# Layer A's query softmax sums and denominators from one pass of products, and whole-array transposes for the last block's output

## The chip, the cores and the metric

The kernel runs on one NeuronCore of a Trainium2 chip. Its five engines have queues of their own and meet only through semaphores: PE (TensorE, matrix products into eight PSUM banks), DVE (VectorE), ACT (ScalarE), POOL (GpSimd) and SP (SyncE, which issues nearly all DMAs). An instruction at the head of a queue that waits holds up everything behind it on that engine. The metric is the device time of one execution in microseconds (us); lower is better.

## The reference

The input x has 2048 rows of 512 values. Four residual layers follow one another, A, B, A, B, each x = x + layer(layernorm(x)), with 32 heads of 16 values.

Layer A is linear attention with softmax features:

```python
pq = einsum(q, w_phi); pk = einsum(k, w_phi)
phi_q = concat([softmax(pq), softmax(-pq)]); phi_k = concat([softmax(pk), softmax(-pk)])
kv = einsum("bhsf,bhsd->bhfd", phi_k, v);  z = einsum("bhsf->bhf", phi_k)
den = einsum("bhqf,bhf->bhq", phi_q, z) + 1e-6
o = einsum("bhqf,bhfd->bhqd", phi_q, kv) / den;   out = o @ wo
```

Layer B is local attention: each position looks at 8 positions behind it, two apart, and its output goes through a second matrix `wo`.

Write E0 = exp(pq) and E1 = exp(-pq), S0 and S1 for their sums over a head's 16 features, and D0 and D1 for their sums weighted by z. The denominator is D0/S0 + D1/S1, and what multiplies E0 is rho0 = 1 / (S0 (D0/S0 + D1/S1)). The same number is S1 / (D0 S1 + D1 S0).

## The kernel before

The rows are cut into four blocks of 512 (b = 0 to 3), each of four tiles of 128 (t = 0 to 3); L is 0 or 1 for the first or second pair of layers. The work is written as stages, named for layer, L and b, and each stage is a list of small steps, one list per engine:

- `fold1`, `fold0`: w_phi is folded into the key and query weights at the start (wT holds transposed weights).
- `lnA0..`: first layer norm. `stat` is statistics on VectorE (line 514), `ap` the normalisation, `pt` and `pe` transposes on PE and their copies.
- `a1_Lb` (lines 615 to 690): key products `mk`, exponentials `ek` on ScalarE, value products `mv`, sums over features, normalisation, and `kv`, which adds into one PSUM bank over all four blocks.
- `a2_Lb` (lines 720 to 743): query products `mq`, the exponentials `eq` (E0 and E1 in tiles Eq), then `ms` (32 small products with the 0/1 matrix indS give S0 and S1) and `rs` (their reciprocals by Ln and Exp into rS).
- `akvL` (lines 760 to 779): the copy of kv, four transposes `tr`, and from them ZM (z, spread over 32-column regions) and R. This is the point at which layer A has seen all keys; no denominator can start before it.
- `a3_Lb` (lines 800 to 860): `md`, 32 small products of Eq and ZM, give D0 and D1; `dr` on VectorE multiplies them with rS and adds; `ln` on ScalarE takes the reciprocal (Ln, Exp); `rho` multiplies it with rS. Then rho is spread over the features, for four blocks by small products `bc` with indB and multiplied into Eq (`mulp`, line 838), for the other four through DRAM (`wr`, `rdb`, `muld`).
- `a4_Lb`: numerators (line 923), output product with WoA (line 542), residual sum and norm. A residual sum is done either on VectorE (line 555) or by a fifth product with the identity on PE (545) and a copy on ScalarE (552).
- `b1`, `b2`, `b3`: layer B, with products on VectorE over shifted windows (`prod`, line 1042, and `pav`, line 1104, four of each for a block), sums on PE, and Vg, copies of V that SP's DMAs spread over the partitions.
- The last block of the last layer (L = 1, b = 3) does layer B another way, on PE: `sc`, `mo`, `nrm`, then `b4_13.pt`, which transposes its output with 64 products onto 32-column strips (line 1365), and the output product with WoB, whose rows were loaded in a matching permuted order.

Which step is issued when is not computed in the kernel. A string, `_ORDER`, lists step after step as base-36 numbers of the lists; each number issues the next step of that list. A second string, `_CHOICE`, says for each flexible step (a PSUM eviction, a normalisation, a residual sum) which engine does it, and `_SLOTS` which buffer each tile takes. What made them is not in the file. The constants that GpSimd makes (line 210 on: masks, cleared ZM tiles, ones) are issued ahead of the string and are not in it. Each engine then executes its own instructions strictly in the order of the string.

Of the kernel before, what the change touches and what calls it, by code (L numbers as in the profile page):

```python
# [8 lines left out]
BF16 = mybir.dt.bfloat16  # L9
# [7 lines left out]
P = 128  # L17
NJ = 16
D = 512
# [31 lines left out]
    "rho_pad": 0,  # L51
# [9 lines left out]
8 2 i 2e 3s e3 ce 2p 23 i a 5l i i 9 i i i 5o i i i i 4e e7 1m i 0 3u 3r 0 f i e c j b 2 k 3 4 j o 5q 1m l 3 m  # L61
p 1n 0 i 1 n 1t e4 o 1o q 1m 1p r 0 1m 1u s 1m z 5k z z 5 1m 1r 7 6 z 20 20 7 1q 1s 1t 21 21 t 20 20 1v 22 10
z 22 1t 7 1t 20 1w 22 t 11 24 24 13 u 12 16 12 1t t 15 1t v 12 12 22 x 18 14 1x d w w 1y 2c y 18 18 26 18 2d
1f 2d 2c 1z 2d 24 2d 27 17 19 18 1a 1b 21 1c 1d 22 21 22 39 1e 20 20 22 39 25 2c 3b 3a 3a 1f 3a 2d 3a 2f 2c 1f
1f 39 ch 22 2f 2d 2g 1g 29 1f 2d 1j 2f 2d 7 1h 29 1i 1k 3a 29 2n 29 2i 2n 3c 2o 2o 2o 2k 2o 2k 2q 1l cd 2h 2n
2a 2k 2f 2n 2k 3a 2o 2j 24 2q 2r 2q 2o 2o 2o 29 2y 28 2y 2y 3c 2l 2z 2v 2z 2s 2z 2z 2k 2y 2z 39 36 31 2z 36 2z
3a 3b 36 36 2v 31 2v 37 2v 31 2t 36 2z 36 2b 2b 2b 2b 2m 2m ci 36 36 2m 3a 2w 2m 2v 33 34 32 31 3c 35 2q 3c 36
3b 2x g 2x 2u 2x 30 37 2x 36 38 38 38 38 3i 3c 3h 3c 39 3b 3a 3j 3k 3k 3k 3c 3d 3c 3e 3l 3b 3m 3d 3e 5h 3n 3m
3c 3e 3e 3l 5i 3m 3q 3m 3m 4f 3m 3d 3l 5j 3e 3e 3m 5i 3m 3m 3v 3d 3e 3e bd 5h 5m 5n 5i 5i 5i 3m 3d 3e 7c 5h 7d
5p 5i 5i 5i 5r 3f 3g 3g 5i 3f 3g 5i 3w 3f 3z 3x 3f 3g 5s 3y 7e 40 41 3g 7d 5u 5v 7f 5t 3g 3p 41 42 41 41 44 3g  # L70
43 3g 43 5w 5x 5x 7f 45 46 43 43 47 43 7f 5y 3f 90 47 48 49 3g 4c 91 5x 41 4b 41 41 41 4a 92 5x 4d 60 91 4l 5z
61 5z 93 5z 4q 62 5z 4g 7d 4g 4g 4m 4q 63 ck 5z 7d 4r 93 4i 4l 63 66 64 67 7g 4s 7j 65 7h 7i 4h 4j 7k bo 4n 4q
4q 4u 4w 91 7l 4t 7l 7l 7m 7l 7o 68 7n 7n 4l 7p 3h 7n 7q 4w 93 4v 7n 4v 3o 91 4f 6a 7r 4o 6b 7n 6k 6f 69 4g 4k
4l 7r 6l 7s h 4w 6g 6k 6m 4p 6a 6c 6p 7t 7u 6a 6k 6f 6n 7v 4w 6k 6h 94 6r 6d 4x 4x b2 6r 4x 97 6o 98 4x 95 6f
# [22 lines left out]
if fh ig gb if ig gg ig gl gs ge gs fg ig gk gb gp gt gr gr gr gt ga gf ih ih if ig if ig du gr if if gs ih du  # L97
# [13 lines left out]

_SLOTS = {
    "med": (
        "b79ca642352f85de6b0464b12833892cb7516e70efd8561f1706ed4a53bc7430e3f9eba731f9cd011a4091d20483b8ae4c4f"
        "b71d6236f9ec40bfd6ea7830c4"
    ),
    "ps": (
# [1979 lines left out]
```

## Time and profile before

| | |
|---|---|
| three runs | 321.89, 321.91, 322.22 us; median 321.91 |
| the profiled execution | 321.75 us, of it 320.0 us between the first and the last instruction |
| PE busy | 307.5 us of the span |
| VectorE busy | 295.9 us |
| ScalarE busy | 274.9 us |
| granted TensorE clock, mean | 0.998 |
| moved by DMA | 36.37 MB |

How to read the lines that follow. A group line gives source line, engine, operation, output and input tiles with their shapes, how many (x), then the busy time in us, the mean duration of one in ns, and the idle time of that engine just before them with what ended it. A timeline line gives start, duration, engine, line and operation; the bracket at its end is idle time before it. A line of a stretch gives for each engine the busy time in it (and how many instructions began), then the granted clock, DMA share and GB/s. PE's durations overlap, because its products are pipelined.

### The profile page before, as it was taken

The page shows a single profiled execution, that of the slowest core. Times are in us where ns is not written, and L with a number is a line of the kernel's source. Part 1 is how long each engine was busy: PE and PEld are TensorE (multiplying, and loading weights), DVE is VectorE, ACT ScalarE, POOL GpSimd, SP SyncE. Part 2 cuts the span into 40 slices and gives each one's busy share as a digit, 9 for nine tenths or more (in the row PEclk, how much of TensorE's full clock was granted, in tenths as well). Part 3 has the DMA queues.
Part 4 walks back from the last instruction along what each step waited for, and adds up shares of the span by engine and source line. Part 5 has one row for each costly group of instructions (what it writes and reads, how often), then busy time and mean ns, then how long its engine had stood idle before and what let it go on. Part 6 is the DMA issues. An engine that isn't in the chain of part 4 may idle for free. (4 is left out here: it accounts for less than half of the span.)

```text
span 320.0 us, 8889 instructions
## 1 busy us (share of the span) xinstructions
PE 307.5 (96%) x3572; PEld 152.2 (48%) x3572; DVE 295.9 (92%) x458; ACT 274.9 (86%) x638; POOL 47.5 (15%) x64
## 2 busy tenths in 40 slices
PE   7999999899999999999999999879999999999993
PEld 3554456445454444444444455544444444444541
DVE  5999996998999999999999999599997999999993
ACT  4999999999898778999999999799999777698560
POOL 6000000000004121000000000041240744035000
PEclk9999999999999999999999999999999999999999
DMA  6977100005794979948994500014389855567733
GB/s 200 349 193 148 35 2 4 2 18 148 177 160 110 152 134 142 137 83 120 153 132 54 69 0 2 4 39 113 89 171 137 151 120 126 133 159 158 182 137 103
DMA packets 45789, 36.37 MB, mean 114 GB/s; under 512 B 30832, under 2 KB 41136, under 8 KB 45744
## 3 DMA queue, kind: packets, MB, share of 16 engines
q1 hardware_dynamic: 45216, 35.75, 55.8%
q8 instruction: 29, 0.48, 0.7%
q14 instruction: 16, 0.13, 0.2%
q10 hardware_dynamic: 528, 0.02, 0.1%
HBM read 11.13 MB, written 3.25 MB: 45 GB/s over the span
## 5 line engine op out<-in xcount | busy, mean ns | idle before, releaser
L950 PE MATMUL PS<-xnT,WB 128*128 128x512 bf16 x336 | 76.8, 379 | 0.1
L1042 DVE TENSOR_TENSOR prod<-QT,K 128x4096 bf16<-128x4096 bf16 x28 | 63.4, 2286 | 0.5 <-POOL K L976 0.5
L1104 DVE TENSOR_TENSOR pav<-PT,Vg 128x4096 bf16<-128x4096 bf16 (+1 forms) x29 | 62.9, 2215 | 0.2
L950 PEld LDWEIGHTS <-WB 128*128 128x128 bf16 x336 | 37.4, 114 | 36.3 <-issue 3.3
L728 ACT ACTIVATE Eq<-PS 128x512 bf16<-128x512 f32 x64 | 36.3, 619 | 0.0
L621 ACT ACTIVATE Ek<-PS 128x512 bf16<-128x512 f32 x64 | 35.1, 622 | 0.2 <-PE PS L615 0.2
L542 PEld LDWEIGHTS <-oT 128*128 128x128 bf16 x240 | 22.3, 98 | 27.1 <-issue 1.3
L720 PE MATMUL PS<-xnT,WA 128*128 128x512 bf16 x128 | 32.0, 380 | 0.5 <-DVE s L812 0.3
L562 ACT ACTIVATE sqd<-x 128x512 bf16<-128x512 bf16 x48 | 30.0, 635 | 2.2 <-DVE x L555 2.0
L555 DVE SCALAR_TENSOR_TENSOR x<-PS,x 128x512 bf16<-128x512 f32 x47 | 30.9, 684 | 1.0 <-PE PS L542 0.9
L627 PE MATMUL PS<-WA,xnT 128*128 128x512 bf16 x128 | 31.6, 379 | 0.0
L615 PE MATMUL PS<-WA,xnT 128*128 128x512 bf16 x128 | 30.7, 379 | 0.0
L204 ACT CAST oT<-PS 128x512 bf16<-128x512 f32 (+1 forms) x50 | 26.9, 599 | 4.3 <-PE PS L1113 2.6
L542 PE MATMUL PS<-WoA,oT 128*128 128x512 bf16 x128 | 29.8, 380 | 0.0
L542 PE MATMUL PS<-WoB,oT 128*128 128x512 bf16 x112 | 27.3, 379 | 0.0
L204 ACT CAST K<-PS 128x512 bf16<-128x512 f32 x30 | 17.3, 594 | 3.0 <-PE PS L950 1.9
L615 PEld LDWEIGHTS <-xnT 128*128 128x128 bf16 x128 | 12.4, 98 | 14.8 <-issue 0.4
L627 PEld LDWEIGHTS <-xnT 128*128 128x128 bf16 x128 | 12.2, 98 | 14.5 <-issue 0.4
L673 DVE TENSOR_TENSOR Ek<-Ek,rk 128x4096 bf16<-128x4096 bf16 (+1 forms) x10 | 18.6, 1860 | 0.4 <-ACT rk L668 0.4
L720 PEld LDWEIGHTS <-WA 128*128 128x128 bf16 x128 | 11.6, 98 | 14.6 <-issue 1.7
L465 DVE TENSOR_SCALAR xn<-x,rstd,nmr 128x512 bf16<-128x512 bf16 x48 | 17.9, 420 | 0.6
L204 ACT CAST V<-PS 128x512 bf16<-128x512 f32 x26 | 15.2, 596 | 2.6 <-PE PS L950 2.6
(164 smaller groups left out, 501.2 us busy)
## 6 DMA issues: line engine op xcount, KB each, us to landing
Vg<-V SPq DMA_DIRECT2D x112, 131.5 KB, 4.3
Prho<-rd SPq DMA_DIRECT2D x8, 512.0 KB, 5.7
x<-in_A_x_dram SPq DMA_DIRECT2D x3, 512.0 KB, 6.8
WB<-in_B_wqkv_dram SPq DMA_DIRECT2D x3, 512.0 KB, 9.9
out_dram<-x SPq DMA_DIRECT2D x6, 256.0 KB, 2.5
wraw<-in_A_wqkv_dram SPq DMA_DIRECT2D x4, 256.0 KB, 4.3
vd<-Vs SPq DMA_DIRECT2D x2, 272.0 KB, 3.0
x<-in_A_x_dram SPq DMA_DIRECT2D x4, 128.0 KB, 3.6
```

The costliest lines, as they stand in the source:

```text
L204: self.nc.scalar.copy(out=out, in_=in_)
L542: nc.tensor.matmul(y[:], lhsT=lh(t, c), rhs=Wo()[:, c, :], start=(c == 0), stop=(c == NB - 1 and not onpe))
L555: nc.vector.scalar_tensor_tensor(out=xb[:, t, :], in0=T[t][:], scalar=1.0, in1=xb[:, t, :], op0=ALU.mult, op1=ALU.add, **kw)
L562: nc.scalar.activation(out=sqd[:], in_=xb[:, t, :], func=ACT.Square, accum_out=T["ss"][:, t:t + 1])
L615: nc.tensor.matmul(pk[:], lhsT=xnT[:, t, k, :], rhs=self.WA[:, k, D:2 * D], start=(k == 0), stop=(k == NB - 1))
L621: nc.scalar.activation(out=T["E"][:, t, s, :], in_=T["k", t][:], func=ACT.Exp, scale=1.0 - 2.0 * s)
L627: nc.tensor.matmul(pv[:], lhsT=xnT[:, t, k, :], rhs=self.WA[:, k, 2 * D:3 * D], start=(k == 0), stop=(k == NB - 1))
L720: nc.tensor.matmul(pq[:], lhsT=self.WA[:, k, hb * P:(hb + 1) * P], rhs=xnT[:, :, k, :], start=(k == 0), stop=(k == NB - 1))
L728: nc.scalar.activation(out=self.Eq[L, b][s][:, :, hb, :], in_=T[hb][:].rearrange("p (t i) -> p t i", t=4), func=ACT.Exp, scale=1.0 - 2.0 * s)
L950: nc.tensor.matmul(pp[:], lhsT=self.WB[:, k, i * D + c:(i + 1) * D:NB], rhs=xnT[:, :, k, :], start=(k == 0), stop=(k == NB - 1))
L1042: nc.vector.tensor_tensor(out=pr[:], in0=QT[:, c:c + 1, :].to_broadcast([P, NW, TB]), in1=win, op=ALU.mult)
L1104: nc.vector.tensor_tensor(out=pv, in0=PT[:, :, lo:lo + n].unsqueeze(1).to_broadcast([P, NB, 2, n]), in1=vw, op=ALU.mult)
```

## The change

S0, S1, D0 and D1 now come out of one set of 32 products. ZM's regions get, beside the eight columns of z, eight columns of the 0/1 head mask, so that `md` yields sums and denominators in neighbouring groups of eight rows of one whole bank M. `ms` and `rs` go. `neg` (ScalarE) copies one half of M to SBUF, `cross` (VectorE) multiplies the two halves, `mn` (PE) adds each pair of row groups with a fixed matrix `pairs`, `ln` takes the reciprocal of 256 instead of 128 columns, and `rho` (VectorE) multiplies all of M, 512 columns, with it. The 1e-6 is added in halves to z, when kv is copied. The mask columns are written into both ZM tiles by `ind_s`, at the start, where it used to fill a tile of its own. rho's layout has sums and (unused) denominators side by side, so the write to DRAM carries 512-byte instead of 256-byte pieces.

In the last block `pt` makes 4 instead of 16 products per tile, on the whole array, and the output product reads B_wo in natural row order; a new DMA, `lwn`, loads it into WoA when layer A no longer needs that tile. The halo product `hv` runs over all 128 columns, and its copy reads the upper 64 rows.

`_ORDER`, `_CHOICE` and `_SLOTS` are new from end to end. Read out, the new order holds at four places:

- Start, VectorE: small, ind_av, zero, ind_qk, mask_h, ind_s, stat(0), phi, mask_2, stat(1). ScalarE: fold1.ev(0), two ln, ap(0), fold1.ev(1). PE: five warm-up products, fold1.tr(0), seven more, fold1.tr(1), two more. (Before, VectorE: zero, mask_h, small, ind_av, ind_qk, ind_s, stat(0), phi; both fold1.ev on VectorE; eleven warm-up products first.)
- akv0, PE: last kv, a2_01.mq(3), tr, a2_02.mq(1), md of block 0, md of block 1, mn of block 0, mn of block 1, a2_02.mq(2), bc of block 0. ScalarE: neg of block 0, one Exp, neg of block 1, both ln. VectorE: cross, cross, R, rho, rho, mulp.
- akv1, PE: last kv, a2_12.mq(3), tr, a2_13.mq(0), md of blocks 0 and 2, mn, mn, a2_13.mq(1), bc. ScalarE: three Exps, neg, one Exp, neg, ln, ln. VectorE: copy of kv, ZM, cross, R, cross, rho, rho, mulp.
- End, VectorE: the last two half-size pav, one residual sum of the last block, four of block 2.

```diff
         def ind_s():
-            nc.vector.memset(self.indS[:], 0.0)
-            for hb in range(NB):
-                nc.vector.tensor_copy(out=self.indS[:, hb, hb * 8:(hb + 1) * 8], in_=self.maskH[:])
+            m = self.maskH[:]
+            msk = bass.AP(m.tensor, m.offset, [list(m.ap[0]), [0, 2], [0, 2], [1, 8]])
+            for zm in self.ZM:
+                for s in range(2):
+                    o = zm[:, s * 72:s * 72 + 1]
+                    dst = bass.AP(o.tensor, o.offset, [list(o.ap[0]), [128, 2], [48, 2], [1, 8]])
+                    nc.vector.tensor_copy(out=dst, in_=msk)
...
-        def ms():
-            T["S"] = S = self.ps()
...
-        def rs():
-            r = self.sm([2, P], "rS", F32, 4)
-            nc.scalar.activation(out=r[:], in_=T["S"][:, 0:2 * P], func=ACT.Ln)
-            nc.scalar.activation(out=r[:], in_=r[:], func=ACT.Exp, scale=-1.0)
-            self.rS[L, b] = r
...
         def ev(dve):
-            self.copy(dve, self.kvT[:], self.kvp[L][:])
+            if dve:
+                nc.vector.tensor_scalar(out=self.kvT[:], in0=self.kvp[L][:], scalar1=self.heps_t[:, 0:1], scalar2=None,
+                                        op0=ALU.add)
+            else:
+                nc.scalar.activation(out=self.kvT[:], in_=self.kvp[L][:], func=ACT.Identity, bias=self.heps_t[:, 0:1])
...
         def md():
-            T["D"] = Dp = self.ps()
+            T["M"] = Mp = self.ps()
             for s in range(2):
                 for hb in range(NB):
+                    lo = (hb % 2 * 2 + s) * P
                     for t in range(4):
-                        nc.tensor.matmul(Dp[32 * t:32 * t + 32, s * P:(s + 1) * P],
+                        nc.tensor.matmul(Mp[32 * t:32 * t + 32, lo:lo + P],
                                          lhsT=zm[:, self.reg(s, hb) * H:(self.reg(s, hb) + 1) * H],
...
-        def dr():
-            r = self.rS[L, b]
...
+        def neg():
+            T["Mn"] = self.sm([2, P], "Mn", F32)
+            nc.scalar.copy(out=T["Mn"][:], in_=view()[:, :, 1, :])
+
+        def cross():
+            T["U"] = self.sm([2, P], "U", BF16)
+            nc.vector.tensor_tensor(out=T["U"][:], in0=view()[:, :, 0, :], in1=T["Mn"][:], op=ALU.mult)
+
+        def mn():
+            T["N"] = self.ps()
+            nc.tensor.matmul(T["N"][:, 0:2 * P], lhsT=self.pairs[:], rhs=T["U"][:].rearrange("p k i -> p (k i)"),
+                             start=True, stop=True)
 
         def ln():
-            nc.scalar.activation(out=T["Ds"][:], in_=T["Ds"][:], func=ACT.Ln, bias=self.deneps_t[:, 0:1])
-            nc.scalar.activation(out=T["Ds"][:], in_=T["Ds"][:], func=ACT.Exp, scale=-1.0)
+            o = T["Mn"][:].rearrange("p k i -> p (k i)")
+            nc.scalar.activation(out=o, in_=T["N"][:, 0:2 * P], func=ACT.Ln)
+            nc.scalar.activation(out=o, in_=o, func=ACT.Exp, scale=-1.0)
 
         def rho():
-            T["rho"] = self.sm([2, P], "rho", BF16)
-            nc.vector.tensor_tensor(out=T["rho"][:], in0=self.rS[L, b][:],
-                                    in1=T["Ds"][:].unsqueeze(1).to_broadcast([P, 2, P]), op=ALU.mult)
+            T["rho"] = self.sm([2, 2, P], "rho", BF16)
+            nc.vector.tensor_tensor(out=T["rho"][:].rearrange("p s k i -> p k s i"), in0=view(),
+                                    in1=T["Mn"][:].unsqueeze(2).to_broadcast([P, 2, 2, P]), op=ALU.mult)
...
-                nc.tensor.matmul(pp[0:64, :], lhsT=xp[:, 3, k, 64:128], rhs=self.WB[:, k, 2 * D:3 * D],
+                nc.tensor.matmul(pp[:], lhsT=xp[:, 3, k, :], rhs=self.WB[:, k, 2 * D:3 * D],
...
         def pt(t):
             U[t] = self.ps()
-            for q in range(NB):
-                for c in range(NB):
-                    nc.tensor.matmul(U[t][32 * c:32 * c + 32, q * P:(q + 1) * P],
-                                     lhsT=self.oB[L, b][:, t, 4 * q + c::DH],
-                                     rhs=self.ident[:].rearrange("p (r q) -> p q r", r=2), start=True, stop=True,
-                                     tile_position=(0, 32 * c))
+            for c in range(NB):
+                nc.tensor.matmul(U[t][:, c * P:(c + 1) * P], lhsT=self.oB[L, b][:, t, c * P:(c + 1) * P],
+                                 rhs=self.ident[:].rearrange("p (r q) -> p q r", r=2), start=True, stop=True)
...
+        def lwn():
+            nc.sync.dma_start(out=self.WoA[:], in_=self.B_wo.rearrange("(c p) n -> p c n", p=P))
+
+        add("ld_wn", "SP", lwn)
```

More of the change, by code (lines that the diff above doesn't have):

```diff
@@ L155, in __init__ @@
         self.ntile = {t: 0 for t in _KINDS}
[L156 removed]
+        for n in ("xn", "xnT", "oT", "Eq", "kvp", "K", "QT", "Vg", "PT", "vh", "ET", "oB"):
             setattr(self, n, {})
@@ L860, in s_a3 @@
         add(st, "PE", md)
-        add(st, "DVE", dr)
+        add(st, "ACT", neg)
+        add(st, "DVE", cross)
+        add(st, "PE", mn)
         add(st, "ACT", ln)
```

171 lines of the change are left out of this document (83 added, 88 removed).

## The prediction

> **What bounds the kernel now.** I read the page's busy shares first, then busy time in stretches of 10 us, then the timeline of four places (start, the two hand-overs inside layer A, end), and the groups of instructions for prices.
>
> ```profile
> span 320.0 us, 8889 instructions
> ...
> PE 307.5 (96%) x3572; PEld 152.2 (48%) x3572; DVE 295.9 (92%) x458; ACT 274.9 (86%) x638; POOL 47.5 (15%) x64
> ```
>
> ```profile
> 0.00:10.00 10.00, 8.22 (x62) 4.37 (x62) 6.61 (x24) 4.68 (x10) 5.32 (x33) 1.00 0.78 234
> ...
> 30.00:40.00 10.00, 10.00 (x48) 4.54 (x47) 9.86 (x11) 9.91 (x22) 0.00 (x0) 1.00 0.29 54
> ...
> 120.00:130.00 10.00, 10.00 (x71) 4.81 (x70) 10.00 (x6) 8.49 (x19) 1.45 (x2) 1.00 1.04 140
> ...
> 200.00:210.00 10.00, 8.66 (x278) 5.50 (x276) 6.24 (x16) 8.27 (x19) 0.00 (x0) 1.00 0.02 3
> ```
>
> No engine bounds the whole. From 20 to 50 us PE runs full matmuls back to back (48 in 10 us, 0.208 us each). In layer B VectorE has no gap (10.00 of 10). At 200 to 210 nothing is full, and the same at 50 to 60: this is the hand-over in layer A, where the key/value sums must become tiles ZM and R before any denominator can start, and VectorE idles almost 4 us. So the time is: start, PE stretch, hand-over, VectorE stretch, again for the second layer, and a tail. A saving counts only by the engine that is full where it lies.
>
> **Prices of what goes and comes** (count x duration; the busy column is the product with overlap taken out).
>
> ```profile
> L950 PE MATMUL PS<-xnT,WB 128*128 128x512 bf16 x336 | 76.8, 379 | 0.1
> ...
> L555 DVE SCALAR_TENSOR_TENSOR x<-PS,x 128x512 bf16<-128x512 f32 x47 | 30.9, 684 | 1.0 <-PE PS L542 0.9
> ...
> L838 DVE TENSOR_TENSOR Eq<-PS,Eq 128x512 bf16<-128x512 f32 x18 | 11.7, 684 | 0.0
> ...
> L481 PE MATMUL PS<-ident,xn 128*128 128x128 bf16 x80 | 5.7, 220 | 0.1
> ...
> L736 PE MATMUL PS<-Eq,indS 128*32 128x128 bf16 x256 | 5.0, 220 | 0.0
> ...
> L823 DVE TENSOR_TENSOR rho<-rS,Ds 128x256 bf16<-128x256 f32 x8 | 3.4, 421 | 1.9 <-ACT Ds L819 1.9
> ...
> L812 DVE TENSOR_TENSOR s<-PS,rS 128x256 f32<-128x256 f32 x8 | 3.4, 420 | 1.6 <-ACT Eq L728 0.8 <-PE PS L804 0.5 <-ACT rS L743 0.3
> ...
> L742 ACT ACTIVATE rS<-PS 128x256 f32<-128x256 f32 x8 | 3.2, 395 | 0.6 <-PE PS L736 0.6
> ...
> L1365 PE MATMUL PS<-ident,oB 128*32 128x128 bf16 x64 | 2.8, 289 | 0.0
> ...
> L819 ACT ACTIVATE Ds<-Ds 128x128 f32<-128x128 f32 x8 | 2.5, 310 | 0.3
> ...
> L815 DVE TENSOR_TENSOR Ds<-s 128x128 f32<-128x128 f32 x8 | 2.3, 293 | 0.3
> ```
>
> PE: ms goes, 5.0. mn comes, 256 columns, twice an L481 matmul (5.7/80 = 0.071): 8 x 0.14 = 1.1. The last block's transposes fall from 64 at 2.8 to 16 at 0.071 = 1.1. The new choice string sends five more residual sums of layer B through PE and ScalarE (42 instead of 47 on VectorE): 5 x 76.8/336 = 1.1. PE in all -5.0 + 1.1 - 1.7 + 1.1 = -4.5.
> VectorE: dr's two go, 8 x 0.713 = 5.7; cross comes at L812's price, 3.4; rho doubles to 512 elements out of PSUM, L838's shape, 8 x (0.684 - 0.421) = +2.1; five residual sums less, -3.4; other choices, counted in the two strings, are three PSUM evictions less (-2.1), two transposed-tile copies more (+1.4), two normalisations more (+0.8); new constants +0.3. In all about -3.3.
> ScalarE: four small steps a block go and three come, each between L819's 0.31 and L742's 0.40: by these ends -1.8 to -3.8; more evictions and residual sums in its choices give back 1.6: about -1.2 on the nearer end. So every engine's list gets shorter, by some 1.5%, 1.1% and 0.4%.
> The halo product over 128 instead of 64 columns of weights streams the same 512 columns: nothing. The write of rho has twice the bytes (128 KB instead of 64 KB a block) and, in the four blocks that write it, stands 9 us or more of listed VectorE work ahead of its use: nothing, covered by that work; without the cover it would cost at most its landing again, 2.1 us a block by the row below. The new load of B_wo (512 KB) is issued when VectorE has 38 us of listed work to do before the first product that reads it; it hides behind that. Behind it on SP's queue stands a Vg read, with 19 us of VectorE's list ahead of its use. Were it late it would be by the 8.0 us of the WoA load at most.
>
> ```profile
> rd<-rho SPq DMA_DIRECT2D x8, 64.0 KB, 2.1
> ...
> WoA<-in_A_wo_dram SPq DMA_DIRECT2D x4, 128.0 KB, 8.0
> ```
>
> **The start, where a wait is added.** The new ind_s no longer fills a tile of its own; it copies into both ZM tiles, which GpSimd clears only after all its masks. In the new order ind_s stands on VectorE's queue right ahead of the first statistics.
>
> ```profile
> 2.36 0.45 DVE L280 COPY indS<-maskH 128x8 bf16<-128x8 bf16 x4
> ...
> 4.72 0.69 DVE L514 BATCH_NORM_STATS2 stat<-x 128x6 f32<-128x512 bf16 x1 [1.91 <-DMA x<-in_A_x_dram]
> ...
> 5.04 0.56 POOL L240 MEMSET ZM<- 128x256 bf16 x2
> ...
> 5.55 0.66 DVE L273 TENSOR_TENSOR PHI<-phis,maskH 128x512 bf16<-128x512 bf16 x1
> ...
> 6.43 0.81 ACT L467 ACTIVATE xn<-x,nmr,rstd 128x512 bf16<-128x512 bf16 x1 [0.23 <-DVE nmr L456]
> ...
> 8.28 0.63 PE L395 MATMUL PS<-PHI,wT 128*128 128x128 bf16 x4
> ...
> 9.91 1.58 ACT L204 CAST WA<-PS 128x512 bf16<-128x512 f32 x3
> ...
> 10.98 1.89 PE L615 MATMUL PS<-WA,xnT 128*128 128x512 bf16 x8
> ...
> 11.34 1.07 ACT L204 COPY wT<-PS 128x1024 bf16<-128x1024 bf16 x1
> ```
>
> ZM is clear at 5.60, four copies take 0.45, so the first statistics start at 6.05 instead of 4.72: +1.3. Queued behind them: statistics (0.69 and a short closing step) 0.85, PHI 0.66, the second statistics 0.85 (8.5), ScalarE's two small steps 0.5 (4.72 + 0.85 to 6.43 holds them and one of VectorE today, 0.86) and its normalisation 0.8 (9.8), and only then, on ScalarE, the second wT copy, 1.07 (10.9), which stands on VectorE today. The fold products then start near 10.9 instead of 8.28, their four evictions (0.53 each) end near 13.7, and the first full key product starts near 13.0 instead of 10.98: +2.0. From there PE has no gap until the hand-over, so what starts late stays late; its list to the last kv product is 0.3 longer by the new order, but the transposes behind it are no longer behind an ms and its neighbours (0.7): 2.0 + 0.3 - 0.7 = **+1.6** at the hand-over's transposes.
>
> **The hand-over of layer 0.** Today the chain is md, dr (2), ln (2), rho:
>
> ```profile
> 54.10 0.63 PE L804 MATMUL PS<-Eq,ZM 128*32 128x128 bf16 x32
> ...
> 54.85 0.42 DVE L812 TENSOR_TENSOR s<-PS,rS 128x256 f32<-128x256 f32 x1 [0.79 <-ACT Eq L728]
> ...
> 56.41 0.42 DVE L823 TENSOR_TENSOR rho<-rS,Ds 128x256 bf16<-128x256 f32 x1 [0.81 <-ACT Ds L819]
> ...
> 57.80 1.28 DVE L838 TENSOR_TENSOR Eq<-PS,Eq 128x512 bf16<-128x512 f32 x2
> ...
> 204.94 0.40 PE L766 MATMUL PS<-ident,kvT 128*128 128x128 bf16 x4 [0.68 <-ACT kvT L204]
> ...
> 209.03 1.28 DVE L838 TENSOR_TENSOR Eq<-PS,Eq 128x512 bf16<-128x512 f32 x2
> ```
>
> md ends at 54.73, rho at 56.83: 2.1 us. The new chain md, neg, cross, mn, ln (2), rho is 0.40 + 0.42 + 0.22 + 0.80 + 0.68 with about 0.1 at each of five hops (54.73 to 54.85 today): 3.0, 0.9 more. The new order sends the chains of two blocks through together, so the second block's rho is done as well when the first product starts. Counting VectorE's idle time from the transposes to the first product: 2.35 before, 2.65 after: **+0.3**.
>
> **VectorE's list from there to its last pav** is 2.3 us shorter (the -3.3 less 0.7 that lies behind that pav and 0.3 in front): **-2.3**, in full, since it is the full engine there.
>
> **The hand-over of layer 1** is barer today: the first product follows 4.1 us behind the transposes' start. In the new order a full query product stands between transposes and md (0.85), neg waits behind three Exps of ScalarE, and both rhos precede the first product: I get 6.3 us from the last kv product against 4.75, of which 0.8 us is work done ahead: **+0.75**.
>
> **The tail.**
>
> ```profile
> 309.28 1.22 DVE L1104 TENSOR_TENSOR pav<-PT,Vg 128x2048 bf16<-128x2048 bf16 x1
> ...
> 310.42 1.28 DVE L555 SCALAR_TENSOR_TENSOR x<-PS,x 128x512 bf16<-128x512 f32 x2
> ...
> 312.70 2.70 DVE L555 SCALAR_TENSOR_TENSOR x<-PS,x 128x512 bf16<-128x512 f32 x4 [0.55 <-PE PS L542]
> ```
>
> Last pav to last residual sum: 310.50 to 315.40, 4.9 us. The new order has five sums there instead of six, and four of the output's partial products ahead of the last mo: 5 x 0.675 = 3.4: **-1.5**.
>
> Sum: 1.6 + 0.3 - 2.3 + 0.75 - 1.5 = -1.15. The profiled execution took 321.75 us (the span and 1.75 around it), 0.16 below the median of 321.91. 321.75 - 1.15 = 320.6; I say **320.5**, 0.4% under the median. (A measurement of this kernel tells about 0.2%, 0.64 us, from no change.)
>
> **A rule weighed against a row.** Most warm-up matmuls of the start are slow:
>
> ```profile
> 1.34 4.12 PE L308 MATMUL PS<-kvT 128*128 128x512 bf16 x11 [1.34 <-DVE kvT L263]
> ```
>
> ```profile
> L308 PE MATMUL PS<-kvT x14: 379/560/634, 1.3 to 7.5; 128*128 128x512 bf16 x14
> ```
>
> The first eleven are 4.12/11 = 0.375 us apart, later ones like L950's 0.229. The new order starts them later (the cleared kvT stands behind ind_av, near 2.1 us) and breaks them after five. If the slow stretch of some 4.1 us moved onto the first key products, it would cost 4.1 x (1 - 0.229/0.375) = 1.6 us. The Trainium skill, "TensorE: Matmul & The Clock Gate", Part 1, says just this: the array runs at half its clock until it has been busy for a window of about 3.4 us, and falls back after an idle window; by that rule a broken warm-up is at risk, while the granted clock of the row 0 to 10 above reads 1.00 throughout and does not show it. I keep it as a rival, since ten us lie between first warm-up and first key product.
>
> **Rivals.**
> 1. Slower: the longer chain is exposed in the other six blocks too. Each exposure is the 0.9 us above, as VectorE stands still at cross or rho while neg waits in ScalarE's queue. For it: L823 idles 1.9 us today, in front of it ScalarE's Ds. Against: those blocks have more work listed between the steps. Three exposures more make 320.5 + 2.7 = 323.2, all six 325.9; from the third on the kernel is slower.
> 2. Faster: the late start is absorbed, because the list puts query products ahead of it and ScalarE has 3.6 us less in the stretch behind. Without the 1.6, and with the second hand-over free: 318.2; with PE's -4.5 in full 317.4. Against: PE's unbroken stretch.
> 3. No change: the clock's slow stretch falls on the key products, 320.5 + 1.6 = 322.1.
> 4. B_wo arrives late, at most 8 us, 328; 38 us of cover speak against it.
>
> **How the numbers follow.** Forecast 0.42 (its own range 318.7 to 321.2), rival 2 0.14, rival 3 0.12, rival 1 0.30, rival 4 0.02. Faster is forecast and rival 2, 0.56; same is rival 3, 0.12; slower 0.32. The range takes in 317.0 and two thirds of rival 1: to 324.2.
>
> **What would show it.** First statistics near 6.05 with GpSimd's ZM as releaser; first key product near 13.0; the last kv of layer 0 some 1.5 to 2 us later than now; the rho chain 3.0 us long; no ms; VectorE's busy time down by about 3 us; last pav to last sum near 3.4 us; the B_wo load landed long before its use. Wrong if the start costs nothing, if VectorE waits at cross or rho in more than four blocks, or if the first matmuls behind 13 us are slow.

## The result, and the profile after

The changed kernel takes **328.96 us** in the median of four runs (328.63 to 329.35); four runs of the kernel before, taken with them, gave 321.90 (321.86 to 322.22). The ratio is **1.0216, 95% interval 1.0201 to 1.0232**: slower by 7.1 us, where 320.5 was forecast with a range up to 324.2. The profiled execution took 328.63 us, 326.9 of it span.

The head of the page of the changed kernel (busy time by engine, share of the span, instructions), and its group of normalisations on VectorE, then that group in the kernel before:

```profile
span 326.9 us, 8305 instructions
...
PE 306.2 (94%) x3281; PEld 149.5 (46%) x3281; DVE 295.9 (91%) x445; ACT 275.3 (84%) x637; POOL 47.0 (14%) x64
...
L476 DVE TENSOR_SCALAR xn<-x,rstd,nmr 128x512 bf16<-128x512 bf16 x50 | 20.9, 471 | 0.3
```

```profile
L465 DVE TENSOR_SCALAR xn<-x,rstd,nmr 128x512 bf16<-128x512 bf16 x48 | 17.9, 420 | 0.6
```

VectorE has 13 instructions less and the very same busy time, 295.9 us, so all of the 6.9 us of longer span is, for this engine, idle time: 31.0 instead of 24.1. But the list had been forecast to be 3.3 us shorter, and the mean normalisation, which the change does not touch, takes 471 ns, against 420 before.

To find where the time went I lined up the same steps of both lists by their start (us). The last two columns belong to experiments below. Each column is one profiled execution; the one of e6, 322.25 us, is the shortest of its five, 1.4 us under their median.

| step, by its start on VectorE | before | after | e1 | e6 |
|---|---|---|---|---|
| layer 0: first product with rho behind the hand-over | 57.80 | 59.14 | 59.17 | 59.14 |
| layer 0: first query-key product of layer B | 83.94 | 83.85 | 83.88 | 83.85 |
| layer 0: last pav | 174.03 | 173.01 | 173.05 | 173.01 |
| layer 1: first weighting of the keys (Ek) | 182.84 | 186.88 | 183.79 | 183.74 |
| layer 1: first query-key product of layer B | 240.02 | 242.88 | 239.85 | 239.81 |
| layer 1: first pav, second block | 275.05 | 277.74 | 274.95 | 274.73 |
| layer 1: first pav, third block | 298.61 | 305.88 | 303.09 | 300.59 |
| layer 1: last half pav | 309.28 | 316.85 | 314.07 | 310.46 |
| span | 320.0 | 326.9 | 324.2 | 320.5 |

The new kernel is 1.3 us behind at the first hand-over, level at 84 us and 1.0 us ahead at 173. Then there are two steps down: 5 us between 173 and 187, and 4.6 us between 275 and 306. First the earlier place, in the timeline of the changed kernel (start, duration, engine, line; the bracket is idle time before it and what ended it):

```profile
176.21 3.51 POOL L1158 MEMSET Qbd<- 128x4096 bf16 x1 [46.26 <-PE PS L1124]
...
176.45 4.20 DVE L476 TENSOR_SCALAR xn<-x,rstd,nmr 128x512 bf16<-128x512 bf16 x3
180.57 0.68 DVE L201 CAST oT<-PS 128x512 bf16<-128x512 f32 x1
...
181.31 2.98 PE L553 MATMUL PS<-WoB,oT 128*128 128x512 bf16 x13 [2.90 <-DVE oT L201]
```

Three normalisations take 4.20 us, where three elsewhere in the same trace (at 189.51) take 1.06. Beside them GpSimd fills a buffer of the last block with zeros, 3.51 us long. It had waited 46.26 us for that buffer and got it 0.24 us before VectorE began. Behind the normalisations stands a copy for which TensorE waits 2.90 us. In the kernel before, this filling lies at 230.05; only its last 0.65 us meet normalisations, three of which take 1.44 us there. The other 2 of the 5 us are work that the new order puts ahead of Ek; they are won back by 240 us (column e1).

Then the later place:

```profile
268.11 7.43 SPq L1236 DMA_DIRECT2D Qbd<-Qs  x8
...
277.53 0.53 SPq L1242 DMA_DIRECT2D vd<-Vs  x1
278.12 2.43 SPq L1022 DMA_DIRECT2D Vg<-V  x4
...
268.24 3.51 POOL L1158 MEMSET Qbd<- 128x4096 bf16 x1 [7.83 <-PE PS L1060]
...
280.19 0.58 ACT L203 CAST QT<-PS 128x512 bf16<-128x512 f32 x1 [4.36 <-DMA vd<-Vs]
...
281.35 2.29 DVE L1053 TENSOR_TENSOR prod<-QT,K 128x4096 bf16<-128x4096 bf16 x1 [1.32 <-ACT K L203]
```

The same copy of QT in the kernel before, without a wait:

```profile
279.67 0.59 ACT L204 CAST QT<-PS 128x512 bf16<-128x512 f32 x1
```

Read the timeline of the changed kernel from its end. VectorE waits for a copy of K. That copy stands on ScalarE's queue behind a copy of QT, and QT waits 4.36 us: its buffer is one that still holds Vs, and the transfer that reads Vs (`vd<-Vs`) is issued only at 277.53, since it stands on SP's queue behind eight transfers into the second zeroed buffer, whose filling ends at 271.75. ScalarE stands still for these 4.36 us and VectorE for 1.32. Between the first pav of the second block and that of the third, VectorE idles 2.88 us (28.14 us with 25.26 busy; before, 23.56 and all of it busy). The other 1.7 of the 4.6 us are work that the new order puts into this stretch.

A third thing stands behind it. TensorE stops twice, and the profile shows nothing that it waits for ("issue"):

```profile
301.67 0.38 PE L556 MATMUL PS<-x,ident 128*128 128x512 bf16 x1 [0.56 <-issue]
...
307.33 0.20 PE L1332 MATMUL PS<-WA,et 128*8 128x68 bf16 x2 [1.18 <-issue]
```

### The profile page after: what moved, and what is told of

It reads as the page before. It is cut to its first block, busy times and chain, and to the rows that moved or that the text cites. A ratio compares the mean times of both kernels' runs of the same rounds, so it can differ in the third digit from the quotient of the medians.

```text
span 326.9 us, 8305 instructions
## 1 busy us (share of the span) xinstructions
PE 306.2 (94%) x3281; PEld 149.5 (46%) x3281; DVE 295.9 (91%) x445; ACT 275.3 (84%) x637; POOL 47.0 (14%) x64
## 4 chain that ended last, share of the span: by engine, by line
PE 63%; ACT 14%; DVE 10%; SPq 4%; issue 4%; DMA 2%; POOL 1%; DVEq 0%; ACTq 0%; POOLq 0%
PE PS L553 14%; PE PS L961 14%; PE PS L638 7%; PE PS L626 6%; PE PS L731 5%; PE PS L1060 3%; DVE prod L1053 3%; DMA Vg<-V 2%; PE PS L701 2%; ACT sqd L573 2%; ACT Eq L739 2%; SPq L1022 2%; PE PS L1181 2%; ACT x L563 2%; DVE xn L476 2%
## 5 line engine op out<-in xcount | busy, mean ns | idle before, releaser
L626 PE MATMUL PS<-WA,xnT 128*128 128x512 bf16 x128 | 30.3, 379 | 0.0
L638 PE MATMUL PS<-WA,xnT 128*128 128x512 bf16 x128 | 30.1, 379 | 0.0
L566 DVE SCALAR_TENSOR_TENSOR x<-PS,x 128x512 bf16<-128x512 f32 x42 | 27.7, 684 | 2.2 <-PE PS L553 2.0
L476 DVE TENSOR_SCALAR xn<-x,rstd,nmr 128x512 bf16<-128x512 bf16 x50 | 20.9, 471 | 0.3
L203 ACT CAST QT<-PS 128x512 bf16<-128x512 f32 x26 | 15.5, 596 | 5.6 <-DMA vd<-Vs 4.4
L1003 POOL COPY vh<-V 128x64 bf16<-128x64 bf16 x6 | 8.5, 1420 | 72.5 <-ACT V L203 68.6
```

The lines of the kernel that those rows point to most:

```text
L203: self.nc.scalar.copy(out=out, in_=in_)
L566: nc.vector.scalar_tensor_tensor(out=xb[:, t, :], in0=T[t][:], scalar=1.0, in1=xb[:, t, :], op0=ALU.mult, op1=ALU.add, **kw)
L626: nc.tensor.matmul(pk[:], lhsT=xnT[:, t, k, :], rhs=self.WA[:, k, D:2 * D], start=(k == 0), stop=(k == NB - 1))
L638: nc.tensor.matmul(pv[:], lhsT=xnT[:, t, k, :], rhs=self.WA[:, k, 2 * D:3 * D], start=(k == 0), stop=(k == NB - 1))
```

## The experiments

All times below are medians and stand against runs of the kernel before on the same chip, whose median was 321.65 to 321.95 in every group. Runs of one variant lie up to 3.5 us apart, so a median of four says little about differences under 1 us; where it matters I compare stretches of the traces.

### e1: the zeroed buffer from elsewhere

The buffers of the kernel are handed out by a string of slots. From the first `Qbd` on, slots 1 and 7 change roles; nothing else differs:

```diff
 "big":
-  ...76076464015231205315264136204275300142
+  ...76016464075237205375264736204215300742
```

> The first zeroed query buffer of the last block takes a big buffer that comes free earlier (the two buffers exchange their roles from there on), so that GpSimd fills it near 168 us, while VectorE multiplies, and not at 176.21, while VectorE normalises. Theory (GpSimd's long memset holds VectorE's bf16 tensor_scalar back): the three normalisations take about 1.06 us in place of 4.20, the first product of the second layer's weighted keys comes 3 to 4 us earlier, and the kernel takes 325.0 to 326.0 us in place of 328.96. Rival (the 4.20 us only fill a wait for what comes next, the order of the list is what costs the time): the normalisations shorten, the end stays within 0.7 us of 328.96. Second rival (the price of those 4.20 us is not the memset): they stay above 3 us.

Measured: **326.14 us** (ratio 1.0126, 1.0085 to 1.0166), 2.8 less than the changed kernel and just above the theory's 325.0 to 326.0. Timeline of e1:

```profile
168.48 3.51 POOL L1158 MEMSET Qbd<- 128x4096 bf16 x1 [38.52 <-PE PS L1124]
...
176.50 1.06 DVE L476 TENSOR_SCALAR xn<-x,rstd,nmr 128x512 bf16<-128x512 bf16 x3
```

The memset costs as much as before, beside VectorE's pav products, and no one notices. The normalisations are back at 1.06, Ek comes 3.09 us earlier, and 2.7 us of it stay won to the end (column e1). VectorE's busy time falls to 292.9. TensorE's wait of 2.90 us is gone too. So the first loss is the meeting of these two instructions.

### e10: half the memset

The dose: the same place, but the zeros written as half as many fp32 elements.

```diff
-            nc.gpsimd.memset(self.Qbd[i][:], 0.0)
+            nc.gpsimd.memset(self.Qbd[i][:].rearrange("p a c t -> p (a c t)").bitcast(F32), 0.0)
```

> The changed kernel, with the two zeroed query buffers written as 2048 fp32 zeros a partition in place of 4096 bf16 zeros, at the same place. Theory (the normalisations wait for as long as GpSimd's instruction lasts): the memset takes about 1.8 us in place of 3.51, the three normalisations 2.4 to 2.6 in place of 4.20, the kernel 1.5 to 1.9 us less than 328.96. Rival (the memset goes by bytes, not by elements): no change.

Measured: 326.03 us (ratio 1.0117, 1.0092 to 1.0143). Timeline:

```profile
176.23 1.80 POOL L1158 MEMSET Qbd<- 128x2048 f32 x1 [46.28 <-PE PS L1124]
...
176.47 2.49 DVE L476 TENSOR_SCALAR xn<-x,rstd,nmr 128x512 bf16<-128x512 bf16 x3
...
278.39 0.59 ACT L203 CAST QT<-PS 128x512 bf16<-128x512 f32 x1 [2.65 <-DMA vd<-Vs]
```

The filling is 1.71 us shorter and the normalisations are 1.71 us shorter. VectorE waits for as long as GpSimd's instruction lasts. The end gained more than the 1.5 to 1.9 that was expected (2.9 us in the median). The second filling, on which SP's queue waits, was halved as well: QT's wait fell from 4.36 to 2.65, and the stretch between the first pav of the second and of the third block from 28.14 to 26.46 us.

### e4: which forms exclude each other

A kernel of its own, of which only the forms matter:

```python
for f in (scale, copy, prod, evict, pscale):      # VectorE, 128x512 each
    for k in range(8):
        f(k)
    nc.vector.tensor_copy(out=z[:, 0:8], in_=y[:, 7, 0:8])
    nc.gpsimd.memset(z[:], 0.0)                   # 128x4096 bf16
    for k in range(8, 16):
        f(k)
```

> Only a measurement, nothing of the layers is computed: VectorE runs five forms on 128x512 (scale and shift of bf16 from SBUF, copy of bf16 from SBUF, product of two bf16 tiles in SBUF, copy out of PSUM, scale out of PSUM), eight of each while GpSimd is idle and eight that begin with a GpSimd memset of 128x4096; then a product of 128x4096 on VectorE with a GpSimd copy of 128x64 beside it. Theory (a GpSimd memset and a VectorE form that reads and writes only SBUF with one tensor input exclude each other): the first scale and the first copy beside the memset take up to 3.5 us longer, the product and the two PSUM forms stay within 0.1 us, and the GpSimd copy beside the product ends with the product, some 2 us late. Rival (the memset slows every form on SBUF by sharing): the product is longer too, and no single instruction takes all of the delay.

Its timeline, VectorE first, then GpSimd:

```profile
9.64 2.99 DVE L27 TENSOR_SCALAR y<-x,sc 128x512 bf16<-128x512 bf16 x9
...
12.61 5.61 DVE L27 TENSOR_SCALAR y<-x,sc 128x512 bf16<-128x512 bf16 x7
...
20.09 1.50 DVE L31 COPY y<-x 128x512 bf16<-128x512 bf16 x7
...
25.88 2.43 DVE L34 TENSOR_TENSOR y<-x 128x512 bf16<-128x512 bf16 x7
...
33.73 4.28 DVE L37 CAST y<-ps 128x512 bf16<-128x512 f32 x7
...
50.90 2.30 DVE L57 TENSOR_TENSOR big<-x 128x4096 bf16<-128x4096 bf16 x1
...
12.76 3.70 POOL L46 MEMSET z<- 128x4096 bf16 x1 [3.46 <-DVE z L45]
20.30 4.73 POOL L46 MEMSET z<- 128x4096 bf16 x1 [3.83 <-DVE z L45]
26.09 3.51 POOL L46 MEMSET z<- 128x4096 bf16 x1 [1.05 <-DVE z L45]
...
51.06 2.23 POOL L58 COPY g<-x 128x64 bf16<-128x64 bf16 x1 [1.10 <-DVE g L56]
...
56.28 0.24 POOL L58 COPY g<-x 128x64 bf16<-128x64 bf16 x1 [0.51 <-DVE g L56]
```

Alone a scaling takes 2.99/9 = 0.33 us; seven beside the memset take 5.61 instead of 2.33, 3.28 more. The copies were not held: here VectorE was first, and it is the memset that took 4.73 instead of 3.51. Products of two SBUF tiles, copies and scalings out of PSUM go on beside the memset at their own pace (0.35, 0.61 and 0.67 each), with the memset at 3.51. But a GpSimd copy of 128x64, 0.24 us alone, takes 2.23 beside a product of 2.30. The theory holds with one correction, that VectorE can also be the one that holds (the copies were expected to wait); the rival of sharing falls, since the products lost nothing.

The Trainium skill, "SBUF — State Buffer", section "Who interferes with whom", says this: VectorE's fast form of scale and copy with both operands in SBUF takes a port pair that it shares with GpSimd, for the whole instruction, and whoever comes first keeps the other waiting; a product of two SBUF tiles excludes only a GpSimd instruction that reads. The rows agree in each point.

### e2, e3, e7, e6: two obstacles in one place

e2 gives QT another buffer:

```diff
 "med":
-  34532178d62acb568492dac172
+  34532178d62acb561492dac872
```

> The third block's query tile of layer B takes another middle buffer (that of K of the block before it, last read at about 267 us), and the last tile of the last block takes the one that the write of Vs still reads. Theory (ScalarE's list waits 4.36 us for that buffer, and with it the evictions of K and V behind it): that wait is gone, VectorE's 5.16 us of idle time between the first pav of the second block and that of the third fall below 2, the kernel takes 324.4 to 326.0 us. Rival (K and V come late from TensorE's products anyway): ScalarE waits for products in place of the buffer, and the gain stays under 1 us, 328.0 or above.

Measured: 328.34 us (1.0231, 1.0186 to 1.0275): **0.6 less, the rival's time, but not by the rival's reason**, which was that ScalarE would wait for TensorE's products. Timeline of e2:

```profile
277.07 0.59 ACT L203 CAST QT<-PS 128x512 bf16<-128x512 f32 x1
...
285.91 2.29 DVE L1115 TENSOR_TENSOR pav<-PT,Vg 128x4096 bf16<-128x4096 bf16 x1 [2.33 <-DMA Vg<-V]
```

The wait for QT's buffer is gone, and VectorE now stands 2.33 us at the next step, before a transfer that nobody had waited for. The profiled execution also has a fall of the granted clock at 180 us (last section), which the one of the changed kernel has not.

e3 is e1 and e2 together.

> Both exchanges of buffers together. Theory (the two losses are separate, and all of the slow-down): 320.5 to 323.0 us, near the forecast of 320.5. Rival 1 (the first loss, once mended, only lets the second stage wait longer for the same thing, or the other way round): no more than the larger of the two alone, about 325. Rival 2 (a third cause holds the end): above 326.

Measured: 325.91 us (1.0139, 1.0107 to 1.0172), 0.2 below e1. By its median, rival 1 it is: the larger of the two alone. The same wait stands in its timeline:

```profile
264.57 8.00 SPq L1236 DMA_DIRECT2D Qbd<-Qs  x8
...
275.14 3.39 SPq L1022 DMA_DIRECT2D Vg<-V  x4
...
281.49 2.29 DVE L1115 TENSOR_TENSOR pav<-PT,Vg 128x4096 bf16<-128x4096 bf16 x1 [2.23 <-DMA Vg<-V]
```

These four transfers read only V (e6 shows that they can run at 266.61). They stand behind the eight that wait for the zeroed buffer. e6 moves them ahead (one token, `fa`, 31 places earlier in the order), in addition to e3; e7 does the same without QT's buffer.

> Both exchanges of buffers, and the second set of four transfers of V of the second block of layer B moved on SP's queue from behind the eight transfers of the query tile to ahead of them, where SP waits for the zeroed buffer. Theory (with the first obstacle gone VectorE's second pav waits 2.23 us for these transfers, which stand in the queue behind the others): that wait is gone and the kernel takes 2 us less than with the exchanges alone, 1 us or less away from the kernel before. Rival (the next thing in line, the products of TensorE or the evictions of ScalarE, is as late as the transfers were): less than 0.7 us is won.

> The exchange of the zeroed buffer and the move of the four transfers, without the exchange of the query tile's buffer. Theory (two obstacles in one place, each of which hides the other): ScalarE still waits some 4 us for the buffer that the write of Vs reads, and the time is that of the exchange of the zeroed buffer alone within 0.7 us, for which 326 was measured. Rival (the transfers alone were the obstacle): as short as with all three.

> The kernel with both exchanges of buffers and the moved transfers once more, as the comparison for the two that follow. Every theory: 323.6 us within 0.7.

Measured: e6 **323.63 us** (1.0050, 1.0036 to 1.0064), and a second time 323.85 (1.0061, 1.0039 to 1.0083); e7 326.52 (1.0162, 1.0135 to 1.0188). Timeline of e6, then the row of e7 in a fence of its own:

```profile
266.61 2.50 SPq L1022 DMA_DIRECT2D Vg<-V  x4
...
279.14 2.29 DVE L1115 TENSOR_TENSOR pav<-PT,Vg 128x4096 bf16<-128x4096 bf16 x1
...
288.04 2.29 DVE L1115 TENSOR_TENSOR pav<-PT,Vg 128x4096 bf16<-128x4096 bf16 x1 [0.64 <-DMA Vg<-V]
```

```profile
276.98 0.59 ACT L203 CAST QT<-PS 128x512 bf16<-128x512 f32 x1 [4.29 <-DMA vd<-Vs]
```

The transfers fit into SP's wait, and the medians fall by 2.1 to 2.3 us against e3, where QT's buffer alone had won 0.2 and the transfers alone nothing. The traces say it more exactly. From the first pav of the second block to that of the third it takes 28.1 us in e1, 27.6 in e3, 27.7 in e7 and 25.9 in e6 (23.6 before): 0.5 for each step alone and 2.3 for both, since each obstacle hid behind the other. From there to the last half pav it takes 11.0 us in e1, 10.2 in e3 and e7 and 9.9 in e6 (10.7 before). That is the third thing: TensorE's two stops are in e1 as in the changed kernel (0.63 and 1.20 us), the second is 0.37 us in e3 and e7, and e6 has neither. Why they go is not shown. e6's theory was also that the kernel comes within 1 us of the kernel before, and that missed.

### e5 and e9: the wait at the start

The `ind_s` step (one token, `c`) moves on VectorE's list from ahead of the first statistics to about 20 us; e5 does so in the changed kernel, e9 in e8 (next).

> The four copies of the mask into the two zeroed stationaries are moved on VectorE's list from ahead of the first statistics to about 20 us. Theory of the prediction (the start costs 1.6 us all the way): the first statistics begin near 4.7 in place of 5.73 and the end is 1.0 to 1.5 us earlier, 327.4 to 328.0. Rival (the lag of the start had gone by 84 us, where the first product of layer B began 0.08 us before its time in the kernel before): the end stays within 0.5 us of 328.96.

> As the last, and the four copies of the mask behind the first statistics. Theory (the start's lag is taken up by waits ahead of 84 us): the same as without, within 0.5 us. Rival (with the later losses gone the start counts): 1.0 to 1.5 us less.

Measured: e5 329.81 us (1.0240, 1.0213 to 1.0266), 0.85 above the changed kernel and outside both ranges (its profiled execution, too, has a fall of the clock), e9 324.67 (1.0077, 1.0052 to 1.0102) beside 324.39 for e8. The wait at the start costs nothing at the end.

### e11: the last block as before

On top of e6, the second part of the change is undone alone:

```diff
-            for c in range(NB):
-                nc.tensor.matmul(U[t][:, c * P:(c + 1) * P], lhsT=self.oB[L, b][:, t, c * P:(c + 1) * P],
-                                 rhs=self.ident[:].rearrange("p (r q) -> p q r", r=2), start=True, stop=True)
+            for q in range(NB):
+                for c in range(NB):
+                    nc.tensor.matmul(U[t][32 * c:32 * c + 32, q * P:(q + 1) * P],
+                                     lhsT=self.oB[L, b][:, t, 4 * q + c::DH], ..., tile_position=(0, 32 * c))
...
-            nc.sync.dma_start(out=self.WoA[:], in_=self.B_wo.rearrange("(c p) n -> p c n", p=P))
...
-        self.s_out(..., lambda: self.WoA, True, ...)
+        self.s_out(..., lambda: self.WoB, True, ...)
```

> The same, with the last block's output product undone: weights in the order of the other blocks, transposes on quarters of the array (16 of 128x32 in place of 4 of 128x128 for each tile), no load of the weights of its own. Theory (the part is worth nothing, since a tile's transposes take 0.65 us in the one form and 0.67 in the other, and all of the saving that was forecast for the tail was VectorE's sums and the order): within 0.6 us of the kernel it is made from. Rival 1 (the 512 KB on the transfer queues push what stands behind them): 0.7 to 3 us shorter. Rival 2 (the whole-array form saves TensorE's time where it counts): longer by 0.7 or more.

Measured: 323.88 us (1.0067, 1.0047 to 1.0087) beside 323.85. Within the 0.6 us of the theory the second part is worth nothing, either way.

### e8, e12, e13: the rest

e6 is still 1.7 to 2.2 us slower than the kernel before. e8 adds three steps to it: V's last eviction of the third block from VectorE to ScalarE (one character of the choices), the six reads of the written Vs behind the third set of V's transfers on SP's queue, and the last half `mo` two output products earlier.

> The two exchanges and the moved transfers, and three more steps in the stretch that is still longer than in the kernel before (from 275 us to the end): V's last eviction of the third block goes from VectorE (0.68 us) to ScalarE; the third set of transfers of V goes ahead of the six reads of the written Vs on SP's queue, which wait 3.3 us for that write; the last half product with the indicator on TensorE goes ahead of two output products. Theory (the rest of the slow-down is the order of VectorE's and SP's lists after 275 us: 0.6 us of cast, 0.64 us of wait for the transfers, some 0.6 us at the end): 1.2 to 1.9 us less than without the three steps, 321.7 to 322.5 us, the kernel before's 321.9. Rival (TensorE's products of this stretch are the bound): less than 0.5 us is won, 323.2 or above.

e12 is e6 with the zeroed buffers written as fp32, e13 is e12 with the last two of e8's steps.

> The same, with three large zeroed buffers (two of the query, one of V) written as fp32 zeros, half as many elements. Theory (SP's queue waits for the second of them, and everything behind it comes earlier by what the filling is shorter, 1.7 us): 0.5 to 1.5 us shorter, near the kernel before. Rival (the queue has slack there by now): within 0.5 us.

> Both exchanges, the moved transfers, the zeroed buffers in fp32, the third set of V's transfers ahead of the reads of Vs, and the last half product with the indicator ahead of two output products; V's last eviction stays on VectorE. Theory (the eviction on ScalarE was what took the gain back): 322.0 to 322.8 us, 0.6 to 1.4 less than without the last two steps. Rival (TensorE's waits for its own instructions and its clock decide this stretch): 323.0 to 324.5, no change.

Measured: e8 324.39 (1.0078, 1.0048 to 1.0109), e12 323.39 (1.0064, 1.0042 to 1.0087), e13 323.00 (1.0052, 1.0029 to 1.0075). None can be told from e6, and none reaches the kernel before; the theories of e8 and e13, which forecast 0.6 to 1.9 us less, missed, and of e12 neither the theory nor its rival can be told. In e8 the pav at 295.27 starts 1.18 us earlier than in e6, as meant, and then it is lost:

```profile
297.28 0.38 PE L556 MATMUL PS<-x,ident 128*128 128x512 bf16 x1 [1.05 <-issue]
...
303.23 0.20 PE L1332 MATMUL PS<-WA,et 128*8 128x68 bf16 x2 [1.47 <-issue]
...
300.14 0.69 DVE L1088 TENSOR_TENSOR PT<-E,rden 128x1024 bf16<-128x1024 bf16 x1 [2.00 <-ACT rden L1083]
```

TensorE stands still twice, for nothing that the profile shows ("issue"), and VectorE waits 2.00 us for rden, whose sums TensorE makes right behind the first stop. These are the two stops of the changed kernel, in front of the same two instructions; they are also in e1, e5, e9 and e10, and not in e6 or the kernel before. What held TensorE, I could not settle.

## Why the prediction was wrong

**The step that failed** is "VectorE's list from there to its last pav is 2.3 us shorter: -2.3, in full, since it is the full engine there". The list is shorter. With the memset out of the way VectorE's busy time is 292.9 us (e1) or 292.5 (e6), 3.0 to 3.4 less than before, and -3.3 was forecast. But "in full" was taken from stretches of the kernel before, in which VectorE had no gap. The change comes with another order and other buffers throughout, and in that list VectorE no longer has that property. From the first query-key product to the last pav of layer 0, before and after (the columns are the length, then PE, PEld, DVE, ACT and POOL):

```profile
83.94:174.03 90.09, 90.09 (x607) 41.51 (x605) 89.35 (x97) 81.98 (x194) 9.33 (x13) 1.00 0.84 132
```

```profile
83.85:173.01 89.16, 89.02 (x601) 40.83 (x600) 87.02 (x84) 83.58 (x195) 14.78 (x12) 1.00 0.83 136
```

VectorE has 2.3 us less work in the same steps, and the steps take 0.9 us less; the rest became idle time. TensorE is busy all through in both, and the prediction's own row of 120 to 130 us has it at 10.00 of 10 beside VectorE: that VectorE alone set the time there was not shown. Behind 174 us come the two waits, which no term of the sum and no rival had: a GpSimd fill beside VectorE's normalisations (2.8 us), and a buffer and a queue before the third block (2.3 to 2.5 against e1 with both mended). From the first product with rho of layer 0 to the last half pav, the stretch of this term and of the second hand-over, the kernel before takes 251.5 us, the changed one 257.7 and e6 251.3: +6.2 and -0.2, where -2.3 and +0.75 were forecast. Both waits could have been asked of the new order on paper, by who frees the buffer of each fill and of each copy, and what then runs beside it.

**The start, +1.6.** The wait is there. The first statistics begin at 5.73 (forecast 6.05), behind GpSimd's ZM; the first key product at 12.23 (13.0, before 10.98), so the key product's delay is 1.25 us and not 2.0. In the changed kernel's timeline:

```profile
5.33 0.60 DVE L285 COPY ZM<-maskH 128x32 bf16<-128x32 bf16 x4 [2.88 <-POOL ZM L239]
5.73 0.69 DVE L525 BATCH_NORM_STATS2 stat<-x 128x6 f32<-128x512 bf16 x1
...
12.23 2.75 PE L626 MATMUL PS<-WA,xnT 128*128 128x512 bf16 x12
...
56.12 0.42 DVE L817 TENSOR_TENSOR U<-PS,Mn 128x256 bf16<-128x256 f32 x1 [1.55 <-ACT Mn L813]
```

At the hand-over's transposes the new kernel is 0.9 us behind (53.84 against 52.92; +1.6 was forecast), and at the first product with rho 1.34 us (1.6 + 0.3). Little of this lag comes from the start. In e5 the first statistics begin at 4.36 and the first key product at 11.61, and yet the transposes begin at 53.95, no earlier than with the wait; in e9 they begin 0.4 us earlier than in e8. By 83.9 the lag is gone, and e5 and e9 show that the wait is worth nothing at the end. So "what starts late stays late" did not hold even up to the first hand-over. The sum had no place where a lag could be taken up.

**The hand-overs.** Prices were right: cross 421 ns, rho 685. In layer 1 it takes 6.15 us from the last kv product to the first product with rho (e1), against 4.77 before; 6.3 and 4.75 were expected. That first product starts 1.0 us later than before (210.05 against 209.03), but by the eighth one e1 is 0.25 us ahead, so the work done ahead was worth more than the 0.8 us that the +0.75 allowed for it. VectorE waits 3.4 us in all for `neg`, in three places and not in six, so rival 1, with most of the slower chances, is not what happened. All idle time in front of `cross` and `rho` is 4.2 us, where the steps that they replace had 3.5. Slower came by another way.

**Where the sum stood well.** With all of VectorE's 2.3 us counted ahead of it, the forecast gives +0.35 us at layer B's first product of the second layer (1.6 + 0.3 - 2.3 + 0.75). Once the memset is moved, e1 and e6 stand there 0.2 us ahead of the kernel before. That is partly luck: the start's +1.6 is not in it, nor is VectorE's saving in full, and the two misses offset each other.

**The tail, -1.5.** Mis-sized: -0.46. From the end of the last pav to the end of the last residual sum the kernel before took 4.90 us, the changed one 4.44 (318.06 to 322.50). The timeline of after:

```profile
315.71 2.35 DVE L1115 TENSOR_TENSOR pav<-PT,Vg 128x2048 bf16<-128x2048 bf16 x2
...
319.54 0.40 PE L1124 MATMUL PS<-pav,indAV 128*32 128x256 bf16 x8
...
319.65 1.99 DVE L566 SCALAR_TENSOR_TENSOR x<-PS,x 128x512 bf16<-128x512 f32 x3 [0.99 <-PE PS L553]
```

The term was five sums of 0.675 without a gap. There are gaps: the product with the indicator for the last half pav runs only at 319.54, 1.5 us after that pav, behind output products, and VectorE waits for TensorE.

**The list sums of TensorE and ScalarE.** They were not terms of the sum, but rival 2 used one. TensorE's busy time fell by 1.3 us and not by 4.5, ScalarE's rose by 0.4 where about -1.2 was given (the prediction's own numbers, -1.8 and +1.6, give -0.2 on the nearer end). `mn` takes 2.2 us and not 1.1, and the transposes are the largest miss.

**The last block's transposes, TensorE -1.7.** 16 products on the whole array were priced at 0.071 us each. The group of the changed kernel:

```profile
L1375 PE MATMUL PS<-ident,oB 128*128 128x128 bf16 x16 | 2.6, 284 | 0.0
```

2.6 us against 2.8 for the 64 on quarters: -0.2. Rival 4, B_wo late, did not come: the load is issued at 263.63 and first read at 304.04, where no wait stands in front of the reader, and e11 is as fast without it.

**The clock, rival 3.** The granted clock is 1.00 in the profile of after for as long as TensorE works, at the start too. That rival did not come here; something like it came elsewhere (below).

What stays open: the 1.7 to 2.2 us that e6 is behind in its medians. Its first profile has a span only 0.5 us above the kernel before's, its second 2.2, of which a fall of the granted clock is 1.35 (below). In the first, the stretch from the second block's first pav to the last half pav is 35.73 us long in e6 and 34.23 before; 0.6 us of that is a cast of V that VectorE did not have there before, 0.8 is idle time more. The tail behind it is 0.7 us shorter than before. But e8, which takes the cast and the wait for transfers away, is no faster, and what the executions without a profile lose is not known.

## What to carry to other kernels

A saving on the full engine is worth its size only if the new order keeps that engine full: ask of the new list, not of the old profile, which buffer each fill, copy and transfer waits for, who frees it, and what runs beside it. In these runs a GpSimd fill was free beside products and PSUM reads, and beside scalings and copies from SBUF to SBUF whichever came second waited for the other; a bf16 buffer zeroed through fp32 took 1.80 us instead of 3.51, and a fill placed beside products cost nothing. When the mending of one wait wins nothing, look at what stands there now before you drop the theory: two obstacles in one place can hide each other, and a lag early in the kernel may be taken up long before the end. And look at how far runs of one kernel lie apart before you read a median of four as nothing: the traces showed 1.3 us for steps whose medians showed 0.2 or less.

## What the runs showed of the hardware

That VectorE and GpSimd exclude each other by whole instructions was new to me in its size: 3.1 us in a kernel in which GpSimd works 14% of the time (e1, e4).

The second thing is the granted clock. In four of the thirteen profiles of variants of the kernel (e2, e5, e6's second, e10) it falls for a while before TensorE's last product, in none of before and after. Stretches of 2 us of e6's second profile (the last three columns are clock, DMA share and GB/s), and then of e2's:

```profile
214.00:216.00 2.00, 1.19 (x57) 0.81 (x60) 2.00 (x4) 1.89 (x5) 2.00 (x3) 1.00 0.28 90
216.00:218.00 2.00, 1.67 (x39) 0.92 (x27) 2.00 (x5) 2.00 (x6) 1.87 (x1) 0.61 1.02 244
218.00:220.00 2.00, 2.00 (x5) 0.76 (x5) 1.27 (x4) 1.29 (x4) 0.00 (x0) 0.53 0.83 199
```

```profile
180.00:182.00 2.00, 0.66 (x2) 0.28 (x3) 1.97 (x6) 0.00 (x0) 0.22 (x1) 0.67 0.02 3
182.00:184.00 2.00, 2.00 (x6) 0.72 (x5) 1.82 (x4) 1.19 (x3) 0.00 (x0) 0.50 1.12 215
```

A mean of 0.61 and 0.53 over 2 us each is some 3.4 us at half clock ((1 - 0.61) x 2 / 0.5 + (1 - 0.53) x 2 / 0.5). In e6's two profiles the first product of layer B lies at 239.81 without such a fall and at 241.16 with it: 1.35 us. It comes where TensorE has little to do, at the hand-over of the second layer or behind the wait of 2.9 us at 178, but not each time: the first profile of e6 has TensorE busy for the same 1.19 us between 214 and 216 and no fall, and the changed kernel has the wait and no fall. The Trainium skill, "TensorE: Matmul & The Clock Gate", Part 1, has the array at half clock after an idle window of about 3.4 us, until it has been busy for one. The length at half clock agrees; what goes ahead is not a whole idle window here, since TensorE was busy for 1.19 of the 2 us before. Whether such falls make the spread of e6's runs, 322.0 to 325.3 us, is not shown; one is worth less than half of it.
